# A short copy of the lower head's first score matmul, put ahead of the full one behind each P.V batch

## The chip, the cores and the metric

The kernel runs on one core of one Trainium2 chip. The metric is the device time in microseconds (us) of one execution; the time before is the median of three runs.

## What is computed

The inputs are x (2048 x 512), the attention weights `wqkv` and `wo`, and the weights of a feed-forward block. With 32 heads of 16 columns each:

```python
xn = layernorm(x)
q, k, v = split_heads(xn @ wqkv)
s = (softmax(q @ k.T * 16 ** -0.5) @ v) @ wo
h = maximum(xn @ w1 + b1, 0) ** 2
g = silu(h @ w2 + b2)
out = x + s * g
```

Everything is in float32.

## The kernel before

A first part (about 130 us) normalizes x and makes q, k and v. The rest is attention, with the feed-forward block worked in between.

Attention goes over 512 steps: 8 groups of four heads (`qd`), 4 chunks of 512 queries (`qc`), 16 blocks of 128 keys (`kb`). A step has two score pairs, `p` = 0 and 1. A pair is two heads: `hp` = 0 lies on partitions 0 to 63 (the upper head), `hp` = 1 on partitions 64 to 127 (the lower head). `score` (line 503) makes one head's 128 keys x 512 queries with one matmul of 64 rows. TensorE can run the two halves of its rows side by side, so the two heads of a pair run at the same time, as do the two halves of a feed-forward product (`Block.issue`, line 551). Such a couple of matmuls, one on each half, is called a pair below, whatever it computes; one after another they make the steps of TensorE. Each matmul comes with a load of its weights, which the profile lists as LDWEIGHTS on PEld.

The exponentials are taken in two ways. A direct pair (`S` in the row strings below) goes into one of two PSUM tiles named S, of two banks each, and ScalarE reads both heads of it in one ACTIVATE of 128 x 1024 (line 507), from PSUM to the tile P; a third S tile holds the feed-forward sums. An aside (`0`, `1`, or `B` for both heads) goes into the banks `acc` and `lin`, is copied to P by VectorE (line 526), and is exponentiated in place later.

The steps are worked in 64 turns of eight. One turn issues a row of letters, then the P.V batch: `values` (line 850) multiplies the eight steps' P tiles with the values, 64 matmuls of 128 rows and 32 columns, four side by side, which add up in `acc`. `L` is one pair of feed-forward (later: output projection) matmuls, and `/` changes the two halves of that product over, behind a fence on GpSimd. The order on every engine is written out by hand in these rows:

```python
    ORDINARY = "SLLSBLLLSLL0SL1LSLL/SBLLSLL0SL1LSLL0L1SLS"
    TWO_PAIRS = "SLSLBLLSL/SBLLSLL0S1LSEVLLSLLB/SSLL0L1S"
    SHORT = "SLLSBLLLS0S1LL0S1/S0LL1SL0SL1L0LSS1"
```

An ordinary turn's row makes 40 pairs: its S pairs are the pairs 0, 3, 8, 12, 16, 19, 23, 27, 31, 37 and 39, counted from 0. `TWO_PAIRS`, with a small P.V batch of two steps (`V`) within it, is used in the four turns that finish one feed-forward block and begin another; `SHORT` in two turns near the end. The first turn has a row of its own. At the start of a turn, `direct` holds the pairs that are to go through S, in order; `nd` of them are exponentiated in the turn's first part, and two more behind the asides.

`see` (line 1101) reads a cell of the last P tile on ScalarE and VectorE at the start of each turn.

Of the kernel before, what the change touches and what calls it, by code (L numbers as in the profile page):

```python
# [76 lines left out]
def fast_path(tc, sb, banks, env):  # L77
# [6 lines left out]
    mm = nc.tensor.matmul  # L84
# [7 lines left out]
    def t(shape, dt, tag):  # L92

        cnt[0] += 1
        if tag in BUFS:
            turn[tag] = turn.get(tag, -1) + 1
            n = turn[tag] % BUFS[tag]
            p, tag = ps.get(tag), f"{tag}{places[n] if tag == 'S' else n}"
        else:
            p = None  # L100
        return (p or ps.get(tag, sb)).tile(shape, dt, tag=tag, name=f"{tag}_{cnt[0]}")
# [394 lines left out]
    steps = [(qd, qc, kb) for qd in range(NQ) for qc in range(NC) for kb in range(NK)]  # L496
    ptile = {}

    def score(i, p, hp, dst):
        qd, qc, kb = steps[i]  # L500
        k, q = ka[qd, kb // 8], qa[qd, qc]
        r = slice(64 * hp, 64 * hp + 64)
        mm(dst, k[r, p, 128 * (kb % 8):128 * (kb % 8) + 128], q[r, p], start=True, stop=True)  # L503

    def exps(i, p, src):
        if src is not None:
            act.activation(ptile[i, p], src, AF.Exp, scale=SCALE)  # L507

    def place(i, p):
        ptile[i, p] = t([128, 2, 512], FT, f"P{2 * ((i - 1) % 8) + p}")  # L510

    def scores(i, p):

        if i < len(steps):
            sc = t([128, 2, 512], FT, "S")
            place(i, p)
            for hp in range(2):
                score(i, p, hp, sc[:, hp])
            return sc

    def aside(i, p, hp):

        if hp == 0:
            place(i, p)
        score(i, p, hp, sides[hp])
        dve.tensor_copy(ptile[i, p][:, hp], sides[hp])  # L526
# [38 lines left out]
    def lin(*halves):  # L565
        done = False
        if pair[0]:
            for half in halves:
                j = half ^ swapped[0]
                done |= pair[0][j].issue(half, lin_banks[j])  # L570
        return done

    def swap():
        if pair[0]:
            while lin(0, 1):
                pass
            f = pool.memset(note[:, notes[0]:notes[0] + 1], 0.0)  # L577
            notes[0] += 1
            for block in pair[0]:
                tc.add_manual_dep(f.ins, block.last, SYNC, reason="the products so far")  # L580
            swapped[0], fence[0] = 1, f.ins.name

    def end_pair():
        if pair[0]:
            while lin(0, 1):
                pass
            swapped[0], last, pair[0] = 0, pair[0], None
            last[0].evict()
# [21 lines left out]
    def split_piece(eng=None):  # L610
        if at_piece[1] == len(pieces):
            return
        j, layer, m = pieces[at_piece[1]]
        at_piece[1] += 1
        raw, q = raws.pop(0), PAIRS[m][1]
        wf[layer, m] = [t([128, 4, 256], FR, f"wf1{p}0") if layer == 1 else t([128, 2, 512], FR, f"wf2{p}{q}")
                        for p in "hl"]
        split(*wf[layer, m], raw, eng or dve, pool)
        load_piece()
# [203 lines left out]
    def early():  # L823
        open_banks(below, "ps2", "left", (("S0", 1024), ("S1", 1024)))
        for q in range(2):
            exps(0, q, scores(0, q))
# [28 lines left out]
    def values_of(steps_now):  # L855
        for i in steps_now:
            values(i, i == steps_now[0], i == steps_now[-1])

    def finish_early():
        early[0] = t([128, 512], FT, "ou")  # L860
        dve.tensor_copy(early[0], sides[0])
# [99 lines left out]
    def make_on(*which):  # L961
        os = []
        for c, g in which:
            n = 64 if (c, g) == (3, 3) else 128
            u, o = pend.pop((c, g)), t([128, 512], FT, "T")
            dve.tensor_tensor(o[:n], u[:n, 0], u[:n, 1], op=OP.mult)
            h, l = onorm[c, g] = on_tiles(c, g)
            os.append((h[:n], l[:n], o[:n]))
        for h, l, o in os:
            dve.tensor_copy(h, o)  # L970
        for h, l, o in os:
            pool.tensor_tensor(l, o, h.bitcast(FT), op=OP.subtract)
# [52 lines left out]
    for j, c in enumerate(ORDER):  # L1025
        for i in range(2):
            n = per * (j + 1) + i - 1 if j < 3 else LAST + 2 + i
# [41 lines left out]
    def happen(time):  # L1069
        for fn, a in events.pop(int(2 * time), ()):  # L1070
            fn(*a)
# [9 lines left out]
    def rest(i, dst):  # L1081

        group(dst, lambda p: onorm[2, 3][p][:, cut[i]], lambda p: wos[0][p][1][:, 1])

    def end_rest(i, src):

        o = t([128, 512], FT, f"wf2{'hl'[i // 2]}{i % 2}")
        dve.scalar_tensor_tensor(o, src, 0.5, gsb[2, i // 2][:, i % 2], op0=OP.mult, op1=OP.mult)
        rows = out[1024 + 128 * i:1152 + 128 * i]
        if i == 2:  # L1090
            pool.tensor_tensor(o, o, stored[0], op=OP.add)
            sp.dma_start(rows, o)
        else:
            pool.dma_start(rows, o, accum_op=OP.add)
# [3 lines left out]
    def see(i):  # L1098

        last = ptile[i, 1][:1, 1, 511:]  # L1100
        act.copy(seen[:, :1], last)
        dve.tensor_tensor(seen[:, 8:9], last, sides[1][:1, :1], op=OP.max)
# [10 lines left out]
    for n in range(TURNS):  # L1113
        i = 8 * n
        happen(n)
        makes = fill[n][:]
        pair[0] = makes.pop(0)()
        if n:
            see(i - 1)
        pairs = [(k, p) for k in range(i + 1, i + 9) for p in range(2)]  # L1120
        short = n in (LAST, LAST + 1)
        nd = 8 if short else 9
        direct, asides = pairs[:nd] + pairs[14:], pairs[nd:14]
        later, aside_at = [], [0, 0]
        for row in TWO_PAIRS if makes else SHORT if short else ORDINARY if n else FIRST:
            if row == "S":
                k, p = direct.pop(0)
                sc = scores(k, p)
                if k == i + 8:
                    later.append((k, p, sc))  # L1130
                else:
                    exps(k, p, sc)
            elif row == "L":
                lin(0, 1)
            elif row in "01B":
                for hp in (0, 1) if row == "B" else (int(row),):
                    aside(*asides[aside_at[hp]], hp)
                    aside_at[hp] += 1
                if row != "B":
                    lin(1 - int(row))  # L1140
            elif row == "/":
                swap()
                if n == TURNS - 1:
                    make_on((2, 3))
            elif row == "E":
                end_pair()
                pair[0] = makes.pop(0)()
            else:
                values_of(range(i, i + 2))
                finish_early()  # L1150
        for j, (k, p) in enumerate(asides):
            exps(k, p, ptile[k, p])
            if j == 0:
                for fn, a in middle.pop(n, ()):
                    fn(*a)
        for a in later:
            exps(*a)
        if n == TURNS - 1:
            two = t([128, 2, 512], FT, "S")
            rest(0, two[:, 0])  # L1160
        pieces_now = pieces_of[n] if n < len(pieces_of) else 0
        ahead = pieces_now > 0 and n % per in (0, 1, 3, 6, 7, 10, 11)
        while lin(0, 1):
            pass
        if ahead:
            split_piece()
        end_pair()
        if n == LAST + 4:
            gsb.update({(1, i): y[1, i] for i in range(2)})
        if n == TURNS - 1:  # L1170
            end_rest(0, two[:, 0])
        happen(n + 0.5)
        for _ in range(pieces_now - ahead):
            split_piece()
        values_of(range(i + 2 if early[0] else i, i + 8))
        finish(n)
# [5 lines left out]
    zc, r = t([128, 16], FT, "zc"), t([128, 16], FT, "rc")  # L1182
# [15 lines left out]
    for i in range(4):  # L1198
        for j in range(4):
            mm(small[32 * j:32 * j + 32, 0, cut[i]], r[:, 4 * i + j:4 * i + j + 1].broadcast_to([128, 32]), ident,  # L1200
               start=True, stop=True)
# [19 lines left out]
    for j in range(2):  # L1221
        for todo in ((0, 0), (0, 1)), ((1, 0),):
            for i in (2 * j, 2 * j + 1):
                group(lins[i], lambda p: (h, l)[p][:, cut[i]], lambda p: wlast[0][:, p],
                      start=len(todo) == 2, stop=len(todo) == 1, todo=todo)
# [120 lines left out]
```

## Time and profile before

| | |
|---|---|
| time, median of 3 runs | 1213.74 us (1213.39 to 1214.49) |
| the profiled execution: time | 1212.94 us |
| the profiled execution: span, first to last instruction | 1211.2 us |
| granted TensorE clock, mean | 0.998 |
| TensorE matmuls, busy | 1200.1 us (99%) |
| TensorE weight loads, busy | 709.9 us (59%) |
| ScalarE, busy | 1040.8 us (86%) |
| VectorE, busy | 845.4 us (70%) |
| GpSimd, busy | 350.1 us (29%) |
| instructions | 24228 |

PE is TensorE's matmuls, PEld its weight loads, which overlap matmuls; ACT is ScalarE, DVE VectorE, POOL GpSimd. A row of the timeline has the start and the length in us, the engine, the source line, the operation, what it writes and reads, shapes and count; in brackets the idle time of the engine before it and what ended that. Rows of neighbouring instructions of one kind are merged. The ends of matmuls are modelled, so starts are the better guide.

### The profile page before, as it was taken

To read this page: it belongs to the slowest core of one execution; us is meant where nothing else is said; L and a number is where in the kernel's file an instruction comes from. 1 tells how busy PE (TensorE), PEld (TensorE's weight loads), DVE (VectorE), ACT (ScalarE), POOL (GpSimd) and SP (SyncE) were. 2 spreads that over 40 slices of the span, in tenths; PEclk is the share of its full clock that TensorE was granted. 3 is DMA by queue.
4 is the path that set the end of the run, shared out by engine and by line. 5 is a ranking of instruction groups with operands and counts; after the bars stand their busy time and mean duration, and the time that the engine had idled before them with its cause. 6 is when DMAs were issued, how large, how long until landed. Compare 5 with 4: busy or idle time off the path is not lost.

```text
span 1211.2 us, 24228 instructions
## 1 busy us (share of the span) xinstructions
PE 1200.1 (99%) x9877; PEld 709.9 (59%) x9877; DVE 845.4 (70%) x1365; ACT 1040.8 (86%) x1231; POOL 350.1 (29%) x268
## 2 busy tenths in 40 slices
PE   9999999999999999999999999999999999999996
PEld 7888655555565555555555565555555555555553
DVE  7666767575866776757687676677775758777776
ACT  6655689889989889988999988889898889999993
POOL 5756523040312321304032122221230404222222
PEclk9999999999999999999999999999999999999999
DMA  7799914131343222224423133151422233464444
GB/s 290 293 371 322 332 58 137 45 111 44 97 154 109 75 69 85 67 75 149 120 77 111 46 97 85 45 183 42 118 80 80 80 99 79 132 207 151 157 140 103
DMA packets 107576, 154.91 MB, mean 128 GB/s; under 512 B 43386, under 2 KB 57736, under 8 KB 107460
## 3 DMA queue, kind: packets, MB, share of 16 engines
q1 hardware_dynamic: 104804, 144.93, 37.3%
q0 software_dynamic: 2368, 7.87, 2.2%
q8 instruction: 78, 1.28, 0.4%
q10 hardware_dynamic: 288, 0.52, 0.1%
q14 instruction: 38, 0.31, 0.1%
HBM read 103.61 MB, written 49.67 MB: 127 GB/s over the span
## 4 chain that ended last, share of the span: by engine, by line
PE 97%; DVE 1%; DMA 1%; SPq 0%; issue 0%; ACT 0%; DVEq 0%
PE acc L850 36%; PE S L551 28%; PE S L503 14%; PE B L314 5%; PE acc L503 5%; PE B L127 4%; PE lin L503 2%; PE D L314 1%; PE D L252 1%; DMA hl<-gd 0%; PE S L993 0%; PE lin L314 0%; SPq L880 0%; PE acc L314 0%; DMA P<-in_A_x_dram 0%
## 5 line engine op out<-in xcount | busy, mean ns | idle before, releaser
L507 ACT ACTIVATE P<-S 128x1024 f32<-128x1024 f32 x702 | 661.9, 1040 | 93.7 <-PE S L503 91.9
L850 PE MATMUL acc<-P,V 128*32 128x512 f32 x4096 | 453.6, 594 | 0.0
L526 DVE COPY P<-acc 128x512 f32<-128x512 f32 x322 | 222.8, 692 | 139.7 <-PE lin L503 69.2
L507 ACT ACTIVATE P<-P 128x1024 f32<-128x1024 f32 x322 | 315.0, 1090 | 0.0
L850 PEld LDWEIGHTS acc<-P,V 128*32 128x32 f32 x4096 | 126.3, 110 | 285.6 <-issue 265.6
L503 PE MATMUL S<-QA,KA 64*128 64x512 f32 x1404 | 292.0, 405 | 0.0
L526 DVE COPY P<-lin 128x512 f32<-128x512 f32 x322 | 220.6, 685 | 1.5 <-PE lin L503 0.6
L503 PEld LDWEIGHTS S<-QA,KA 64*128 64x128 f32 x1404 | 134.6, 184 | 111.2 <-issue 41.8
L503 PE MATMUL lin<-QA,KA 64*128 64x512 f32 x322 | 126.8, 394 | 0.0
L503 PE MATMUL acc<-QA,KA 64*128 64x512 f32 x322 | 126.6, 393 | 0.1
L120 POOL TENSOR_TENSOR wf1l<-wr,wf1h 128x1024 fp32r<-128x1024 f32 x28 | 68.4, 2442 | 176.9 <-DVE wf1h L116 108.4
L577 POOL MEMSET note<- 1x1 f32 x68 | 6.0, 88 | 383.2 <-PE S L551 381.7
L551 PE MATMUL S<-xl,wf1h 64*128 64x512 f32 x464 | 95.8, 389 | 0.0
L120 POOL TENSOR_TENSOR hl<-T,hh 128x1024 fp32r<-128x1024 f32 x28 | 79.9, 2855 | 52.9 <-DVE hh L116 52.9
L120 POOL TENSOR_TENSOR wf2l<-wr,wf2h 128x1024 fp32r<-128x1024 f32 x28 | 67.2, 2401 | 90.5 <-DVE wf2h L116 90.5
L551 PE MATMUL S<-xh,wf1l 64*128 64x512 f32 x480 | 91.3, 388 | 0.0
L551 PE MATMUL S<-wf2l,hh 64*128 64x512 f32 x448 | 90.3, 390 | 0.0
L876 DVE TENSOR_TENSOR ou<-acc,ou 128x512 f32<-128x512 f32 x31 | 21.4, 692 | 96.8 <-PE acc L850 91.0
L551 PE MATMUL S<-wf2h,hl 64*128 64x512 f32 x448 | 82.9, 388 | 0.0
L551 PE MATMUL S<-xh,wf1h 64*128 64x512 f32 x480 | 77.7, 392 | 0.0
L551 PE MATMUL S<-wf2h,hh 64*128 64x512 f32 x448 | 71.7, 393 | 0.0
L503 PEld LDWEIGHTS acc<-QA,KA 64*128 64x128 f32 x322 | 59.3, 184 | 17.1 <-DVE P L526 2.4
(370 smaller groups left out, 1427.7 us busy)
## 6 DMA issues: line engine op xcount, KB each, us to landing
wr<-in_B_w_dram SPq DMA_DIRECT2D x56, 512.0 KB
QA<-qd SPq DMA_DIRECT2D x128, 128.0 KB
KA<-kd SPq DMA_DIRECT2D x64, 256.0 KB
u<-ud SPq DMA_DIRECT2D x15, 512.0 KB
kd<-P SPq DMA_DIRECT2D x11, 512.0 KB
V<-vd SPq DMA_DIRECT2D x8, 664.0 KB
qd<-P SPq DMA_DIRECT2D x9, 512.0 KB
vd<-P SPq DMA_DIRECT2D x16, 280.0 KB
```

The lines of the kernel that those rows point to most:

```text
L120: leng.tensor_tensor(lo, src, hi.bitcast(FT), op=OP.subtract)
L127: mm(dst, lhs(a, k), rhs(b, k), start=n == 0, stop=n == len(todo) - 1)
L252: nc.tensor.transpose(halves[k // 2][:, k % 2, 128 * j:128 * j + 128], xnorm[c, i][:, j, 128 * k:128 * k + 128], ident)
L314: mm(dst, left[a][:, k], right[b][:, k], start=n == 0, stop=n == 5)
L503: mm(dst, k[r, p, 128 * (kb % 8):128 * (kb % 8) + 128], q[r, p], start=True, stop=True)
L507: act.activation(ptile[i, p], src, AF.Exp, scale=SCALE)
L526: dve.tensor_copy(ptile[i, p][:, hp], sides[hp])
L551: ins = mm(bank, self.lhs(a, k)[r], self.rhs(b, k)[r], start=n == 0 and self.at[other] == 0, stop=n == len(self.todo[half]) - 1 and self.a ...
L577: f = pool.memset(note[:, notes[0]:notes[0] + 1], 0.0)
L850: mm(sides[0][32 * j:32 * j + 32], vq[qd][:, kb, 17 * j:17 * j + 32], ptile[i, j // 2][:, j % 2], start=first, stop=last)
L876: dve.tensor_tensor(ou, sides[0], part[0], op=OP.add)
```

## The change

`score` gets a width `n`, and `scores` a flag `behind`. Where the flag is set, the lower head's matmul of the pair is issued twice: first for the first 64 of its 512 query columns, then for all 512, into the same bank; the second writes over the first. Both have the same weights, and each comes with its load. The flag is set for the first S pair of each turn but the first, that is for the pair that follows a turn's P.V batch: 63 times in all. The value of the flag is worked out behind the pop, so that `len(direct) == nd + 1` holds for the first pair alone.

```diff
-    def score(i, p, hp, dst):
+    def score(i, p, hp, dst, n=512):
         qd, qc, kb = steps[i]
         k, q = ka[qd, kb // 8], qa[qd, qc]
         r = slice(64 * hp, 64 * hp + 64)
-        mm(dst, k[r, p, 128 * (kb % 8):128 * (kb % 8) + 128], q[r, p], start=True, stop=True)
+        mm(dst, k[r, p, 128 * (kb % 8):128 * (kb % 8) + 128], q[r, p, :n], start=True, stop=True)
...
-    def scores(i, p):
+    def scores(i, p, behind=False):
 
         if i < len(steps):
             sc = t([128, 2, 512], FT, "S")
             place(i, p)
             for hp in range(2):
+                if hp and behind:
+                    score(i, p, hp, sc[:, hp, :64], 64)
                 score(i, p, hp, sc[:, hp])
             return sc
...
-                sc = scores(k, p)
+                sc = scores(k, p, n > 0 and len(direct) == nd + 1)
```

## The prediction

> **What bounds the kernel now.** I read the page first, then the list of waits, then the timeline of one ordinary turn, and last its exponentials one by one. From the page, the span, the engines' busy time and the chain that ended last:
>
> ```profile
> span 1211.2 us, 24228 instructions
> ...
> PE 1200.1 (99%) x9877; PEld 709.9 (59%) x9877; DVE 845.4 (70%) x1365; ACT 1040.8 (86%) x1231; POOL 350.1 (29%) x268
> ...
> PE 97%; DVE 1%; DMA 1%; SPq 0%; issue 0%; ACT 0%; DVEq 0%
> ```
>
> TensorE (PE) carries the chain, so time put on its path is paid. But two rows of the waits (total, times, longest) show that it and ScalarE (ACT) hand work to and fro:
>
> ```profile
> ACT P L507 <- PE S L503: 91.9, 73, 2.3
> ...
> PEld S L503 <- ACT P L507: 22.7, 105, 0.8
> ```
>
> The first is ACT idle through each P.V batch until the first score pair of the next turn is made. The second is a score pair held until an exponential frees its bank, 105 times in the 64 turns. So what the first pair loses goes on through ACT too. Here is the start of an ordinary turn (start, length; x2 is the upper and the lower head):
>
> ```profile
> 435.33 0.19 PEld L503 LDWEIGHTS S<-QA,KA 64*128 64x128 f32 x2 [0.84 <-issue]
> 435.33 0.51 PE L503 MATMUL S<-QA,KA 64*128 64x512 f32 x2
> 435.44 0.43 PEld L551 LDWEIGHTS S<-wf2h,hh 64*128 64x128 f32 x4
> 435.67 0.64 PE L551 MATMUL S<-wf2h,hh 64*128 64x512 f32 x4
> ...
> 436.15 0.40 PE L503 MATMUL S<-QA,KA 64*128 64x512 f32 x2
> ...
> 437.31 0.39 PE L503 MATMUL S<-QA,KA 64*128 64x512 f32 x2
> ...
> 438.23 0.40 PE L503 MATMUL S<-QA,KA 64*128 64x512 f32 x2
> ...
> 439.13 0.40 PE L503 MATMUL S<-QA,KA 64*128 64x512 f32 x2
> ...
> 439.74 0.19 PEld L503 LDWEIGHTS S<-QA,KA 64*128 64x128 f32 x2 [0.18 <-ACT P L507]
> 439.81 0.43 PE L503 MATMUL S<-QA,KA 64*128 64x512 f32 x2
> ```
>
> Counting the letters of the ordinary row as pairs from 0, scores stand at 0, 3, 8, 12, 16 and 19: these six S rows. The first pair's record is 0.51 long where others take 0.39 to 0.40: its weights load is not hidden, and the next loads start 0.11 us after it (435.33 to 435.44). That 0.11 is the price of one exposed 128-column load. The pair at 19 waits for ACT. The same turn's exponentials of pairs 0, 3, 8, 12 and 16:
>
> ```profile
> 435.88 1.02 ACT L507 ACTIVATE P<-S 128x1024 f32<-128x1024 f32 x1 [1.51 <-PE S L503]
> 436.80 1.02 ACT L507 ACTIVATE P<-S 128x1024 f32<-128x1024 f32 x1
> 437.75 1.03 ACT L507 ACTIVATE P<-S 128x1024 f32<-128x1024 f32 x1
> 438.67 1.02 ACT L507 ACTIVATE P<-S 128x1024 f32<-128x1024 f32 x1
> 439.58 1.02 ACT L507 ACTIVATE P<-S 128x1024 f32<-128x1024 f32 x1
> ```
>
> Pair 19 takes the bank of pair 12, whose exponential ends at 438.67 + 1.02 = 439.69; the load starts at 439.74, 0.05 later. And that exponential itself began 0.04 after pair 12's matmuls ended (438.23 + 0.40 = 438.63), so in this turn it was PE that timed it, with ACT only just ready. Both paths to pair 19 matter: ACT from the first exponential, and the lower head's own row of matmuls.
>
> **The change part by part.** In each of 63 turns (all but the first) the lower head's work becomes load, 64-column matmul, load, 512-column matmul. Nothing is removed; no DMA, no wait and no other engine's work is added. The 64 columns themselves are an estimate of 64/512 of a step of 0.23, 0.03 us. What costs is the second load, since the matmul ahead of it is too short to cover it. The nearest rows are the 128x128 transposes, each with a load of its own:
>
> ```profile
> 28.03 1.03 PE L252 MATMUL D<-ident,T 128*128 128x128 f32 x8
> ```
>
> ```profile
> L252 PEld LDWEIGHTS D<-ident,T x56: 138/140/143, 12.9 to 94.7; 128*128 128x128 f32 x56
> L252 PE MATMUL D<-ident,T x56: 270/273/273, 13.1 to 94.8; 128*128 128x128 f32 x56
> ```
>
> Eight take 1.03 us, the last being 0.27 long, so seven steps take 0.76: 0.109 each. A short matmul followed by a load on the same rows costs 0.109, near the exposed 0.11 above. I take 0.11 as the lower head's delay at its 512 columns. Its bounds: 0.03, if the load hid wholly, and 0.38, if the load had to wait for a whole short matmul (at most the 0.27 of the rows) and then took its 0.11.
>
> The Trainium skill, page "TensorE: Matmul & The Clock Gate", section "The mechanism", has a rule that speaks against the change: a weights load overlaps matmuls in flight only where the row group differs. By that rule the delay would be the 0.38. The transposes do not bear it out: records of 0.14 and 0.27 on the same 128 rows could not follow each other every 0.109.
>
> The upper head is untouched: its next load can start at its own matmul's start, as now, and is done before its next step. So from pair 0 on the lower head trails by 0.11. This stagger has a use. Pairs 1 to 8 (435.67 to 437.31) take 1.64 / 7 = 0.234 a step; from pair 8 to 16, where the records are 0.40 long for a single 0.39, one head trailing by about 0.01, they take (439.13 - 437.31) / 8 = 0.2275. At the turn's end the trail is larger:
>
> ```profile
> 443.98 0.44 PE L503 MATMUL S<-QA,KA 64*128 64x512 f32 x2
> 444.21 0.44 PE L551 MATMUL S<-wf2h,hl 64*128 64x512 f32 x2
> 444.44 0.44 PE L503 MATMUL S<-QA,KA 64*128 64x512 f32 x2
> 444.80 7.08 PE L850 MATMUL acc<-P,V 128*32 128x512 f32 x64
> 451.81 0.50 PE L503 MATMUL S<-QA,KA 64*128 64x512 f32 x2
> ```
>
> Records of 0.44 are a trail of 0.05, and they step by 0.23. So heads apart step by 0.2275 to 0.23 and heads together by up to 0.234; no row shows a trail of 0.11, and I take 0.2275 for it.
>
> Up to pair 12 the lower head then needs 11 x 0.2275 = 2.50 instead of the 2.56 from 435.67 to 438.23. It gives back 0.06 of its 0.11 and arrives 0.05 late. That is PE's path to the exponential of pair 12.
>
> ACT's path: the first exponential starts 0.11 late. How fast can ACT catch up? A turn with two blocks shows it with no idle time in seven exponentials, and a score pair held:
>
> ```profile
> 402.20 6.52 ACT L507 ACTIVATE P<-S 128x1024 f32<-128x1024 f32 x7 [1.52 <-PE S L503]
> 404.20 0.19 PEld L503 LDWEIGHTS S<-QA,KA 64*128 64x128 f32 x2 [0.37 <-ACT P L507]
> ```
>
> (6.52 - 1.02) / 6 = 0.917 a step. In the ordinary turn the steps are 0.92, 0.95, 0.92, 0.91. Only the second has room: 0.95 - 0.917 = 0.03. So the exponential of pair 12 comes 0.11 - 0.03 = 0.08 late by ACT, 0.05 late by PE; the later decides, 0.08, and pair 19 is released 0.08 late. There its record of 0.43 shows both heads some 0.04 late already; held for 0.08 more, both start on the same release, so the trail is closed, and the rest of the turn runs as now, shifted. The P.V batch starts behind the last matmul and ACT is idle at its end, so nothing more is carried over and nothing given back: 0.08 a turn. Bounds: 0.05, if ACT can step by 0.90 and PE decides; 0.11, if the trailing head gains nothing and ACT nothing.
>
> Other turns: in the four turns with two blocks and the two short ones, ACT is the bound from its first exponential to the first held pair (the row at 404.20), so they pay the whole 0.11. One late turn pays about nothing, as VectorE holds PE before the second bank is needed:
>
> ```profile
> 1145.04 0.18 PEld L503 LDWEIGHTS acc<-QA,KA 64*128 64x128 f32 x1 [0.51 <-DVE seen L1102]
> ```
>
> **Sum:** 56 x 0.08 + 6 x 0.11 = 4.48 + 0.66 = 5.1 us. The profiled execution took 1212.94 us, 1.7 more than its span of 1211.2 and 0.8 under the median of the runs shown, 1213.74. All terms are within the span, so I add them to the median: 1213.74 + 5.1 = 1218.9 us (+0.42%). With 0.05 and 0.11 for the 62 turns: 1216.8 and 1220.6.
>
> **The rivals.**
> *Nothing comes back, or pace is lost.* The trailing lower head slows at a trail of 0.11, which no row shows: at 0.234 or more it brings its whole 0.11 to pair 12, and each further 0.002 a step adds 0.02. 63 x 0.11 = 6.9 us, 1220.7; with 0.13 a turn 1221.9. For it: no such trail was seen. Chance 0.22.
> *The load must wait for the short matmul.* 0.38 at the first pair, less 0.06 by pace and 0.03 at ACT, at most: about 0.32 x 63 = 20 us, 1234. Against it are the transposes. Chance 0.04.
> *The load hides, or does nothing that lasts.* If the lower head loses only 0.03, ACT's room of 0.03 takes it up and PE's path gains 0.03; pair 19 closes the stagger and the time stays: 1213.7, give or take 1. This is also the case in which the change does not do what it says, a second load with the same weights being no load. Against: the page has 9877 loads for 9877 matmuls. Chance 0.12.
> *Faster: the stagger holds.* If pair 19 does not close it, all 38 steps from 435.67 to 444.44 (8.77 us) would run at 0.2275, 8.65 us: a gain of 0.12 a turn, against a lag at the P.V batch of 0.03 to 0.11. It decides where the lag at the end stays under 0.08; with 0.04, 63 x -0.08 = -5 us, 1208.7. Against it: pair 19 is held by ACT in this turn, and a later first exponential holds it longer. Chance 0.08.
>
> **How the numbers follow.** My own case has 0.54 (range 1216.8 to 1220.6). The range leaves out the wait for the short matmul (0.04) and the faster case (0.08), and takes in the other three: 1213.2 to 1222.0. What a measurement of this kernel can tell from no change is about 0.2%, 2.4 us, or 0.04 a turn. Slower by more: 0.54 + 0.22 + 0.04 = 0.80; within: 0.12; faster: 0.08.
>
> **What would show it.** 63 more loads and matmuls on PE (9940). Behind a P.V batch the lower head's 512 columns start 0.11 later than the upper's, and the first exponential 0.11 later after the first load. Steps up to pair 16 near 0.2275. Pair 19's load held for ACT some 0.1 longer than now, and its record with no trail. The ordinary turn 16.56 instead of 435.33 to 451.81 = 16.48. I would be wrong if the first exponential is less than 0.05 late, if pair 19 is not held, or if the trail lives on to the P.V batch.

## The result, and the profile after

The changed kernel takes 1218.32 us (median of 5 runs, 1218.1 to 1219.76), the kernel before 1213.64 us in the same runs. The ratio is 1.0042, with a 95% interval of 1.003 to 1.0053: slower by 4.7 us. The forecast was 1218.9, slower by 5.1. The profiled execution took 1218.1 us, with a span of 1216.3.

The page of the changed kernel, and the rows of its waits that answer to the two shown of before (lines of the code below the edit have moved by two):

```profile
span 1216.3 us, 24354 instructions
...
PE 1205.4 (99%) x9940; PEld 749.7 (62%) x9940; DVE 846.1 (70%) x1365; ACT 1039.8 (85%) x1231; POOL 350.5 (29%) x268
...
PE 99%; DVE 1%; issue 0%; POOL 0%; ACT 0%; POOLq 0%
```

```profile
ACT P L507 <- PE S L503: 98.1, 72, 2.3
...
PEld S L503 <- ACT P L507: 26.8, 128, 0.8
```

There are 63 more matmuls and 63 more loads (9940 for 9877), so the second load with the same weights is made. ScalarE waits 6.2 us longer for score pairs (98.1 for 91.9), and a score pair is now held for an exponential 128 times instead of 105. The same turn as in the prediction, its timeline:

```profile
436.68 0.19 PEld L503 LDWEIGHTS S<-QA,KA 64*128 64x128 f32 x2 [0.84 <-issue]
436.68 0.61 PE L503 MATMUL S<-QA,KA 64*128 64x512 f32 x3
436.79 0.19 PEld L553 LDWEIGHTS S<-wf2h,hh 64*128 64x128 f32 x1
436.79 0.19 PEld L503 LDWEIGHTS S<-QA,KA 64*128 64x128 f32 x1
...
437.01 0.74 PE L553 MATMUL S<-wf2h,hh 64*128 64x512 f32 x4
...
437.48 0.51 PE L503 MATMUL S<-QA,KA 64*128 64x512 f32 x2
...
438.64 0.50 PE L503 MATMUL S<-QA,KA 64*128 64x512 f32 x2
...
439.55 0.50 PE L503 MATMUL S<-QA,KA 64*128 64x512 f32 x2
...
440.46 0.50 PE L503 MATMUL S<-QA,KA 64*128 64x512 f32 x2
...
441.17 0.18 PEld L503 LDWEIGHTS S<-QA,KA 64*128 64x128 f32 x2 [0.19 <-ACT P L507]
441.17 0.50 PE L503 MATMUL S<-QA,KA 64*128 64x512 f32 x2
...
441.51 0.39 PE L503 MATMUL acc<-QA,KA 64*128 64x512 f32 x1
441.51 0.39 PE L503 MATMUL lin<-QA,KA 64*128 64x512 f32 x1
```

At 436.79 two loads begin: the next one of the upper half, and the lower head's second one. From then on the records of a score pair are 0.50 to 0.51 long for a single 0.39: the lower head trails by 0.11, through pairs 3, 8, 12 and 16. Pair 19 is held, and behind it, at 441.51, the two halves start together again. The 0.50 of pair 19 itself is no trail of this kind: in the trace its lower head starts at 441.25, 0.08 behind the upper, and both records end at 441.67. The exponentials of pairs 0, 3, 8, 12 and 16 of this turn:

```profile
437.33 1.03 ACT L507 ACTIVATE P<-S 128x1024 f32<-128x1024 f32 x1 [1.66 <-PE S L503]
438.25 1.02 ACT L507 ACTIVATE P<-S 128x1024 f32<-128x1024 f32 x1
439.18 1.03 ACT L507 ACTIVATE P<-S 128x1024 f32<-128x1024 f32 x1
440.10 1.02 ACT L507 ACTIVATE P<-S 128x1024 f32<-128x1024 f32 x1
441.01 1.03 ACT L507 ACTIVATE P<-S 128x1024 f32<-128x1024 f32 x1
```

Counted from the turn's first load (436.68, before 435.33) they start 0.10, 0.10, 0.08, 0.08 and 0.08 later than before, and pair 19's load 0.08 later (441.17 - 436.68 = 4.49; before 4.41).

Over all turns of these two executions, taking each turn's length from the starts of its first matmul in the two traces: the 53 turns with the ordinary row are longer by 0.0905 on average, 4.80 us together; the four with two blocks by 0.10 to 0.13, 0.45 together; the two short ones by 0.07 and 0.08; two more near the end by 0.09 and 0.07; and one late turn is 0.26 shorter. With 0.2 less outside the turns that makes the 5.1 us between the spans.

Below, a row's delay is given as the mean over the 50 or so ordinary turns of a trace (one execution each), from the starts of the matmuls counted from the turn's first one. At the pair that has the copy, the full matmul's record starts within the copy's, so there the modelled end is taken; the start of the pair behind it agrees within 0.002. For the change: the lower head's row is late by 0.112 at pair 0, 0.106 at pair 3, 0.093 at pair 8, 0.091 at pair 12 and 0.089 at pairs 16 and 19, and the P.V. batch by 0.090.

### The profile page after: what moved, and what is told of

It reads as the page before. It is cut to its first block, busy times and chain, and to the rows that moved or that the text cites. A ratio compares the mean times of both kernels' runs of the same rounds, so it can differ in the third digit from the quotient of the medians.

```text
span 1216.3 us, 24354 instructions
## 1 busy us (share of the span) xinstructions
PE 1205.4 (99%) x9940; PEld 749.7 (62%) x9940; DVE 846.1 (70%) x1365; ACT 1039.8 (85%) x1231; POOL 350.5 (29%) x268
## 4 chain that ended last, share of the span: by engine, by line
PE 99%; DVE 1%; issue 0%; POOL 0%; ACT 0%; POOLq 0%
PE acc L852 37%; PE S L553 29%; PE S L503 15%; PE B L314 5%; PE acc L503 4%; PE B L127 4%; PE lin L503 2%; PE D L314 1%; PE D L252 1%; PE B L683 1%; PE S L995 0%; PE lin L314 0%; PE acc L314 0%; DVE P L1234 0%; PE S L314 0%; DVE P L1229 0%
## 5 line engine op out<-in xcount | busy, mean ns | idle before, releaser
L507 ACT ACTIVATE P<-S 128x1024 f32<-128x1024 f32 x702 | 661.2, 1042 | 100.0 <-PE S L503 98.1
L503 PE MATMUL S<-QA,KA 64*128 64x512 f32 (+1 forms) x1467 | 324.1, 402 | 0.0
L503 PEld LDWEIGHTS S<-QA,KA 64*128 64x128 f32 x1467 | 163.0, 184 | 104.2 <-issue 41.8
L553 PE MATMUL S<-xl,wf1h 64*128 64x512 f32 x464 | 99.5, 389 | 0.0
L553 PE MATMUL S<-wf2l,hh 64*128 64x512 f32 x448 | 93.3, 389 | 0.0
L553 PE MATMUL S<-xh,wf1h 64*128 64x512 f32 x480 | 83.7, 391 | 0.0
L553 PE MATMUL S<-wf2h,hh 64*128 64x512 f32 x448 | 77.3, 393 | 0.0
L553 PEld LDWEIGHTS S<-xh,wf1l 64*128 64x128 f32 x480 | 62.1, 184 | 3.8
```

The costliest lines, as they stand in the source:

```text
L553: ins = mm(bank, self.lhs(a, k)[r], self.rhs(b, k)[r], start=n == 0 and self.at[other] == 0, stop=n == len(self.todo[half]) - 1 and self.a ...
```

## The experiments

All are timed against the kernel before in shared runs (its medians were 1214.04, 1213.84 and 1213.54 us). The theory at the start was the prediction's: an exposed second load of 0.11, carried to pair 19 by the lower head's matmuls and by ScalarE.

### Is it the load or the columns? 16, 256 and 512 columns

```diff
-                    score(i, p, hp, sc[:, hp, :64], 64)
+                    score(i, p, hp, sc[:, hp, :16], 16)    # and 256, 512
```

> The copy has 16 columns instead of 64. Theory (the price is the second weights load, 0.11 us a turn, which no matmul of that length hides): the same as the change, 1218.3 us, within 0.6. Rival (the price is the columns that are streamed): a quarter of the change's 4.7 us, 1214.8.

> The copy has 256 columns. Theory (the lower head loses the longer of the second load, 0.11, and the copy's own columns): 256 columns are half a step of 0.23, 0.115, so nearly the same as 64 columns: 0.09 to 0.10 a turn, 1218.3 to 1219.5. Rival (price by columns): four times 4.7, 1232.

> The copy has all 512 columns. Theory: its second load is now hidden behind the 512 columns, and the lower head trails by one whole step of 0.23; the first exponential comes 0.23 late, 0.02 to 0.03 are given back up to pair 19, 0.20 stay: 62 x 0.20 = 12.5 us, 1226. Rival (price by columns): eight times 4.7, 1251. Rival (price by loads alone): 1218.

| columns | time, us | ratio (95%) | trail at pair 0, us | P.V. batch later, us |
|---|---|---|---|---|
| 16 | 1219.42 | 1.0045 (1.0031 to 1.0058) | 0.112 | 0.093 |
| 64 (the change) | 1218.32 | 1.0042 (1.003 to 1.0053) | 0.116 | 0.090 |
| 256 | 1220.51 | 1.0055 (1.0041 to 1.0068) | 0.121 | 0.104 |
| 512 | 1226.22 | 1.0102 (1.0087 to 1.0118) | 0.234 | 0.195 |

From 16 to 256 columns the trail hardly moves; it stays near the 0.11 of a load as long as the columns take no more. With 512 the trail is one whole step and no more, so the load hides behind the columns. Each copy came with a load of 128 weight columns, so no run separates the load from some other fixed cost of one more load and matmul; that it is the load rests on the transposes' 0.109 and the exposed load's 0.11. In its timeline the copy's step is plain: the upper half goes on at 439.47 with feed-forward work while the lower head starts its pair 0, and pair 19 is held 443.73 - 439.13 = 4.60 behind the turn's start, 0.19 later than before.

```profile
439.13 0.50 PE L503 MATMUL S<-QA,KA 64*128 64x512 f32 x2
439.47 0.39 PE L553 MATMUL S<-wf2h,hh 64*128 64x512 f32 x1
439.47 0.39 PE L503 MATMUL S<-QA,KA 64*128 64x512 f32 x1
```

```profile
443.73 0.19 PEld L503 LDWEIGHTS S<-QA,KA 64*128 64x128 f32 x2 [0.19 <-ACT P L507]
```

The price by columns is refuted. The 512 columns came as expected (1226); 16 and 256 columns took a little more (1219.4 for 1217.7 to 1218.9, and 1220.5 for 1218.3 to 1219.5), but their intervals overlap the change's.

### Does the trail give anything back? A copy for both heads

```diff
-                if hp and behind:
+                if behind:
```

> Both heads get the 64-column copy, so each loses the load and neither trails. Theory (the load is the price, the trail gives back about 0.02): the whole 0.11 a turn, 62 x 0.11 = 6.8 us, 1220.4. Rival (the trail between the heads is what costs): the time goes back to 1213.6. Rival (each extra matmul is paid on TensorE): twice the change, 1223.

1220.01 us, ratio 1.0048 (1.0034 to 1.0061), an interval that holds the change's 1.0042. Both heads lose the load and start together behind it, as the records of four matmuls in 0.62 show; pair 19 is held at 442.89 - 438.40 = 4.49, as in the changed kernel:

```profile
438.40 0.62 PE L503 MATMUL S<-QA,KA 64*128 64x64 f32 x4
438.85 0.62 PE L553 MATMUL S<-wf2h,hh 64*128 64x512 f32 x4
```

```profile
442.89 0.19 PEld L503 LDWEIGHTS S<-QA,KA 64*128 64x128 f32 x2 [0.21 <-ACT P L507]
```

The lower head's row is late by 0.114 at pair 0 and 0.093 at pair 12, the P.V. batch by 0.087 (the change: 0.112, 0.091, 0.090). So the 0.02 that is given back between pair 0 and pair 12 comes without a trail as well. The 1220.4 that I expected here lies near the time, but not for the reason given: the ordinary turns are no longer than with the change, and what the profiled execution has more lies in single late turns (0.4 us) and ahead of the first turn (1.8 us), where nothing was changed. That the trail costs, or that each matmul is paid, is refuted.

### Lower head or first exponential? The copy at pair 27

```diff
-                sc = scores(k, p, n > 0 and len(direct) == nd + 1)
+                sc = scores(k, p, n > 0 and len(direct) == nd - 6)
```

> The copy stands not in the first score pair of a turn but in the eighth (pair 27 of an ordinary turn), whose exponential has 0.2 us of room. Theory (the lower head's own row of matmuls carries the delay; 12 pairs are left to the P.V. batch, with no held pair between): 0.09 to 0.11 a turn stay, 1219.3 to 1220.5. Rival (only the first exponential's delay counts): nothing, 1213.6.

1218.46 us, ratio 1.0039 (1.0025 to 1.0053). All nine exponentials of the turn's first part start within 0.002 of before; the lower head is late by 0.109 at pair 27 and still by 0.097 at pair 39, while the upper head is not late at all, and the P.V. batch is late by 0.090. The trail is seen up to the batch (records of 0.53, before 0.44):

```profile
445.57 0.53 PE L503 MATMUL S<-QA,KA 64*128 64x512 f32 x2
445.80 0.53 PE L553 MATMUL S<-wf2h,hl 64*128 64x512 f32 x2
446.03 0.53 PE L503 MATMUL S<-QA,KA 64*128 64x512 f32 x2
446.48 0.63 PE L852 MATMUL acc<-P,V 128*32 128x512 f32 x3
```

So a late lower row is paid in full without any late exponential. The time is 0.8 us under the range that I gave. In the profiled execution the short turns and two others lose only 0.01 to 0.02 each, about 0.3 us less than the range has for them, and one late turn is 0.27 shorter, which is discussed below; why those four lose so little was not looked into.

### ScalarE alone: one, two and four small copies ahead of the first exponential

```diff
                 sc = scores(k, p)
+                if n > 0 and len(direct) == nd + 1:
+                    for j in range(2):            # and 1, 4
+                        act.copy(held[:, j:j + 1], sc[:1, 1, 511:])
```

(in the kernel before; `held` is a tile of one row)

> The kernel before with one more ScalarE copy of a single cell of the first score pair ahead of its exponential, in 63 turns: TensorE's matmuls are those of before, only ScalarE starts 0.1 to 0.2 late. Theory that ScalarE's path to pair 19 is as tight as TensorE's (room 0.03): 0.07 to 0.15 a turn stay, 1218 to 1223. Rival (only the lower head's row of matmuls decides, ScalarE has room): 1213.6 to 1214.5.

> The kernel before with two one-cell ScalarE copies ahead of the first exponential of 63 turns (one delayed it by 0.054 and cost nothing). Two delay it by about 0.11, as the change did, with TensorE's matmuls as before. Theory (ScalarE steps by 0.905 at best, so it makes up 0.03 before pair 8's exponential and 0.02 before pair 12's): 0.05 to 0.06 of it reach pair 12's exponential and pair 19, 62 x 0.055 = 3.4 us, 1217. Rival (ScalarE has room for all of 0.11, TensorE's row alone makes the change's cost): 1213.7. Rival (ScalarE's delay alone makes the change's cost): 1218.3.

> The same with four copies, a delay of about 0.22. Theory: 0.05 made up, 0.17 reach pair 19: 62 x 0.17 = 10.5 us, 1224. Rival (room for all): 1213.7.

| copies | time, us | ratio (95%) | exponential later at pair 0 / 3 / 8 / 12, us | P.V. batch later, us |
|---|---|---|---|---|
| 1 | 1213.42 | 0.9997 (0.9988 to 1.0006) | 0.054 / 0.051 / 0.020 / 0.002 | -0.001 |
| 2 | 1214.60 | 1.0011 (1.0002 to 1.002) | 0.108 / 0.104 / 0.073 / 0.052 | 0.021 |
| 4 | 1221.35 | 1.0068 (1.0055 to 1.0082) | 0.209 / 0.205 / 0.173 / 0.152 | 0.117 |
| none; the change | 1218.32 | 1.0042 (1.003 to 1.0053) | 0.106 / 0.109 / 0.092 / 0.092 | 0.090 |

With two copies the first exponential is as late as with the change, but the cost is 1.1 us, not 4.7. ScalarE makes up 0.05 by pair 12, since it can step faster than it does in the kernel before, where it steps by 0.92 to 0.95 up to there:

```profile
438.31 0.20 ACT L1132 COPY held<-S 1x1 f32<-1x1 f32 x2 [1.51 <-PE S L503]
438.42 8.28 ACT L507 ACTIVATE P<-S 128x1024 f32<-128x1024 f32 x9
```

Nine exponentials in 8.28, the last 1.06 long: (8.28 - 1.06) / 8 = 0.9025 a step. What is left at pair 12 falls again on the way to the P.V. batch. The first theory (ScalarE's path as tight as TensorE's, one copy costing 0.07 to 0.15 a turn) fell with the first run; the second (0.05 made up) held for the exponentials up to pair 12, but I expected 1217 and 1224 where 1214.6 and 1221.4 came, as up to 0.035 more is taken up behind pair 12.

### Another place for the held pair

```diff
-    ORDINARY = "SLLSBLLLSLL0SL1LSLL/SBLLSLL0SL1LSLL0L1SLS"
+    ORDINARY = "SLLSBLLLSLL0SL1LSLL/BSLLSLL0SL1LSLL0L1SLS"
```

> The kernel before with the letters S and B behind the / of the ordinary row changed over, so that the held score pair stands one step later, at 20. The hold of some 0.04 there goes: up to 52 x 0.04 = 2 us, 1211.6; if the fence behind / is as late as the bank was, nothing: 1213.6.

> The changed kernel with the same two letters changed over. Theory (the lower head's row of matmuls is 0.09 late whatever holds pair 19, and the fence behind / or the P.V. batch waits for it): 0.07 to 0.10 a turn over the swapped kernel without the change, 1216 to 1218.5. Rival (the change costs only through the bank that pair 19 waits for): the same time as the swapped kernel without the change.

Both expectations of the absolute time were wrong: without the change 1218.92 us, ratio 1.004 (1.0027 to 1.0054), with it 1225.15, ratio 1.0091 (1.0077 to 1.0105). In the kernel without the change two other waits take the place of the one removed:

```profile
441.94 0.69 DVE L526 COPY P<-lin 128x512 f32<-128x512 f32 x1
...
442.69 0.18 PEld L503 LDWEIGHTS lin<-QA,KA 64*128 64x128 f32 x1
...
444.53 0.19 PEld L503 LDWEIGHTS S<-QA,KA 64*128 64x128 f32 x2 [0.17 <-ACT P L507]
```

The aside, now at 19, needs its bank `lin`, which VectorE has copied out only at 441.94 + 0.69 = 442.63; the score pair behind it starts late in its lower head, and pair 27 waits for that exponential. On this kernel the change adds 6.2 us, the P.V. batch is 0.096 later than in the swapped kernel without it, and the times of the two have spreads of 1.3 to 1.8 us. So about the same 0.09 goes through another chain of waits, in which no score pair is held at 19. No kernel that was run is faster than the one before by more than its interval.

## Why the prediction was right, and where its steps were not

**The price of the copy: right.** I took 0.11 for the second load, from the transposes' 0.109 and the exposed load's 0.11; the trail is 0.116, and from 16 to 256 columns it is 0.11 to 0.12. The upper head went on as before, as forecast. A rule of the Trainium skill, page "TensorE: Matmul & The Clock Gate", section "The mechanism" (a load overlaps matmuls in flight only in other row groups), would have made it 0.38, if nothing else of that section is taken in: it also has loads to a background weight buffer go ahead of matmuls in flight. The rule by itself does not hold here: the second load begins at 436.79 on the rows of the copy's matmul, whose record runs from 436.68 for 0.29 us, and the trail behind it is 0.11. Whether such a buffer is at work no run shows.

**What the trail gives back: mis-sized.** I took steps of 0.2275 for halves that stand apart, and so 0.06 back by pair 12. Measured: 0.02, with steps of 0.230 in the lower head's row between pairs 0 and 12, both with the trail and with both heads copied (before 0.232). With the copy at pair 27 the lower row steps by 0.2293 from pair 28 to pair 39, before by 0.2305. So stagger and short steps stood together in the rows that I read, but where the trail was set on purpose, at pair 27, the steps are only some 0.001 shorter. What makes the turn's first steps longer than its later ones was not settled.

**Which path decides at pair 19: wrong.** I had ScalarE arrive 0.08 late and the lower head's matmuls 0.05 late. It is the other way round: the lower head's matmuls are 0.09 late at pair 12, and ScalarE, delayed by the same 0.11 on its own, is only 0.05 late there. The step that failed is the 0.917 that I took for ScalarE's own pace. I subtracted the length of the first record, 1.02, from a merged row whose records grow, so the last one counted too long. The second and the last exponential of that row stand five steps apart:

```profile
403.12 1.02 ACT L507 ACTIVATE P<-S 128x1024 f32<-128x1024 f32 x1
...
407.64 1.08 ACT L507 ACTIVATE P<-S 128x1024 f32<-128x1024 f32 x1
```

(407.64 - 403.12) / 5 = 0.904, near the 0.9025 that the run with two copies showed later. With 0.904 the steps of 0.95 and 0.92 in the ordinary turn leave 0.06 of room up to pair 12, not 0.03, and ScalarE arrives 0.05 late, as measured. So in the changed kernel TensorE times that exponential: its matmuls end at 439.55 + 0.50 = 440.05 and it starts at 440.10, 0.05 behind them, as it did before the change (0.04). The pace of the matmuls was taken too fast and that of ScalarE too slow; the two errors have opposite signs and left 0.08 for a measured 0.09. That the total came so near is in this part luck.

**The trail is closed at pair 19: right,** as at 441.51; its mean, from the starts, falls from 0.095 at pair 18 to 0.003 at pair 20; at pair 19 the lower head still starts 0.076 behind, and the two records end together. What was not in the sum is that the hold is no condition of the cost: where no hold follows (the copy at pair 27) the P.V. batch waits for the trailing half.

**The sum.** 56 x 0.08 + 6 x 0.11 = 5.1. Measured: 0.09 in the ordinary turns; 0.10 to 0.13 with two blocks, as forecast; 0.07 to 0.08 in the short turns, not 0.11; and -0.26 in the one late turn where I had nothing. Ahead of that turn's start VectorE had been held by a transfer in the execution before, and not in the one of the changed kernel; the turn's difference from before was between -0.33 and +0.18 in the other traces, also where ScalarE alone was changed, so it is not laid to the change.

**The rivals.** Nothing comes back (1220.7): right in that the lower head's matmuls bring the delay to pair 12, but they do not slow with the trail, and 0.02 of the 0.11 is given back. The hidden load, the load that waits for the whole short matmul, and the stagger that lasts are refuted: a load is made and takes 0.11, and the trail that does last (the copy at pair 27) is no gain.

## What to carry to other kernels

Here a short matmul cost 0.11, with 16 columns as with 64, which is an exposed weights load and not its columns: look for what hides the load, and if nothing does, price it by the nearest exposed load in the trace. To get a step from a merged row, take the starts of single instructions, for the last record may be longer than the first. Where two engines hand work to and fro, do not pick the later one from the steps that each shows in that rhythm, for an engine that is fed just in time shows its feeder's pace; delay one alone by a known amount and see how much of it arrives. And two things that stand together in a trace, such as a stagger and a short step, need not be cause and effect.

## What the runs showed that I had not expected

ScalarE's one-cell copies delay the next exponential by 0.05 each (0.054 for one, 0.108 for two, 0.209 for four), though their records are 0.14 to 0.15 long. In this turn one such copy is free, two cost 1.1 us in 63 turns and four 7.8 us.
